# Attention steps of three score units on rotating pairs of PSUM banks, with a joined value phase for two query chunks, in a fused attention and gated-FFN kernel

## Chip, cores and metric

The kernel runs on one core of a Trainium2 chip. The metric is the time of one execution on the device in microseconds (us). "Before" is the kernel as it was and "after" the changed one. A comparison uses runs of both kernels on the same chip in the same rounds.

## The reference

Eight batches of causal attention (8 heads, 576 queries, 16 extra "beacon" keys that no mask covers, head size 64) are reshaped to 4608 tokens of 512 features and go through a gated feed-forward network (FFN) with 1536 hidden columns.

```python
B, H, S, Nb, D = (8, 8, 576, 16, 64)
scores = scale * np.matmul(q, k_all.transpose(0, 1, 3, 2))      # k_all: beacon keys, then keys
scores = np.where(causal, -1000000000.0, scores)
a = np.exp(scores - scores.max(-1, keepdims=True))
a /= a.sum(-1, keepdims=True) + 1e-09
x = np.matmul(a, v_all)        # then (B, H, S, D) -> (B*S, H*D)
gate = np.maximum(x @ w_gate, 0.0)
out = (gate * (x @ w_val)) @ w_out
```

## The kernel before

Attention of one batch and the FFN of earlier tokens run interleaved, so that TensorE always has matmuls while ScalarE (ACT) does exponentials and VectorE (DVE) multiplies and reciprocals. The work of a batch is cut into 14 score **units**: a tile of two PSUM banks, four to twenty matmuls, one exponential. A batch has seven **steps** of two units. When all units of a query chunk (of 240, 256 or 80 queries) are done, a **value phase** multiplies the exponentials by the values and sums them. Then a quota of FFN groups follows: "up" (four gate matmuls, Relu, four value matmuls, multiply) or "down" (twelve matmuls, copy out). What no batch is left to cover runs at the end as a **tail** of FFN alone, with 24 up groups.

PSUM, the memory that matmuls write to, has eight banks here, shared so: two score pairs (four banks), two banks for a value phase, two single banks for the FFN. The value matmuls of some up groups use the first bank of a score pair (`spare`).

```python
s_ps = main.enter_context(tc.tile_pool(name="s_ps", bufs=2, space=bass.MemoryType.PSUM))
o_ps = main.enter_context(tc.tile_pool(name="o_ps", bufs=1, space=bass.MemoryType.PSUM))
f_ps = main.enter_context(tc.tile_pool(name="f_ps", bufs=2, space=bass.MemoryType.PSUM))

class Unit:
    def qk(self):
        self.s = s_ps.tile([P, 2, 512], FP32, name="s")
        ...                                   # score matmuls into both banks
    def exp(self):
        e = psb.tile([P, 1024], BF16, name="e")
        nc.scalar.activation(e..., self.s..., AF.Exp, scale=scale)
        ...                                   # causal mask on GpSimd where needed

class Ffn:
    def up(self, nf, c0, c1, spare):
        g = f_ps.tile([P, M_TILE], FP32, name="f")
        for ki in range(KM):
            nc.tensor.matmul(g[:, :n], wg[:, ki, nf * P:(nf + 1) * P], x[:, ki], ...)
        gs = fsb.tile([P, M_TILE], FP32, name="g")
        nc.scalar.activation(gs[:, :n], g[:, :n], AF.Relu)
        if spare:
            u = s_ps.tile([P, 2, M_TILE], FP32, name="s")[:, 0]
        else:
            u = f_ps.tile([P, M_TILE], FP32, name="f")
        for ki in range(KM):
            nc.tensor.matmul(u[:, :n], wv[:, ki, nf * P:(nf + 1) * P], x[:, ki], ...)
        nc.vector.tensor_mul(self.h[:, nf, c0:c1], gs[:, :n], u[:, :n])

plan = (... + [(b, i, 2.6 if b == 2 else 4.4) for b in range(2, B) for i in range(7)]
        + [(None, 0, 4.5)])                   # batch, step, FFN quota

for s, (b, i, quota) in enumerate(plan):
    units = [Unit(batches[b], order[2 * i + x]) for x in range(2)]
    for j, u in enumerate(units):
        u.qk()
    units[0].exp()
    values()                                  # value phases that are due
    other = list(units[1:])
    for j, (kind, _, run) in enumerate(mine): # FFN groups within the quota
        run(spare)
        if other:
            other.pop().exp()                 # second exponential after the first group
```

The batches are counted from zero in the code: `b == 2` is the third batch.

Of the kernel before, what the change touches and what calls it, by code (L numbers as in the profile page):

```python
# [10 lines left out]
FP32 = mybir.dt.float32  # L11
# [5 lines left out]
def general_path(tc, q, k, v, beacon_k, beacon_v, out, ident, wg, wv, wo):  # L17
# [79 lines left out]
    with tc.tile_pool(name="gen_sb2", bufs=1) as sb, \  # L97
# [56 lines left out]
        ((g, 0, 0),), ((g, 0, 1), (g, 1, 3)), ((g, 1, 2),), ((g, 1, 1),), ((g, 1, 0),),  # L154
        ((g, 2, 4), (g, 2, 3), (g, 2, 2)), ((g, 2, 1), (g, 2, 0)))
)


@with_exitstack
def kernel(  # L160
# [12 lines left out]
    nc = tc.nc  # L173
# [27 lines left out]
    bounds = [const.tile([P, 256], FP32, name=n) for n in ("least", "most")]  # L201
# [10 lines left out]
    s_ps = main.enter_context(tc.tile_pool(name="s_ps", bufs=2, space=bass.MemoryType.PSUM))  # L212
    o_ps = main.enter_context(tc.tile_pool(name="o_ps", bufs=1, space=bass.MemoryType.PSUM))
    f_ps = main.enter_context(tc.tile_pool(name="f_ps", bufs=2, space=bass.MemoryType.PSUM))
# [111 lines left out]
    UNITS = [(x, t) for t in range(NKT) for x in "kqv"]  # L326
# [24 lines left out]
    class Unit:  # L351
# [9 lines left out]
        def qk(self):  # L361
            self.s = s_ps.tile([P, 2, 512], FP32, name="s")
            for g, _, (kt, q0, n, _, _), c in self.parts:
                (kT, k0), (qT, q0) = self.batch.keys(kt), self.batch.queries(q0)
                for j in range(2):
                    for a in range(2):
                        rows = slice(a * D, (a + 1) * D)
                        nc.tensor.matmul(  # L368
                            self.s[:, a, c + j * n:c + (j + 1) * n],
                            kT[rows, 2 * g + j, k0:k0 + P], qT[rows, 2 * g + j, q0:q0 + n],  # L370
                            start=True, stop=True)
# [17 lines left out]
    class Chunk:  # L389


        def __init__(self, batch, g, ci):
            self.batch, self.g, self.ci = batch, g, ci
            self.last = len(CHUNKS[ci][2]) - 1
            self.turned = batch.b == 0 and ci < 2

        def av(self):
            spare = self.batch.b == 0 and self.g == 1
            if spare and self.ci == 2:
                s = s_ps.tile([P, 2, 2, 256], FP32, name="s")  # L400
                self.ab, self.os = s[:, 0], s[:, 1, 0]
            else:
                self.ab = (f_ps if spare else o_ps).tile(
                    [P, 2, 256], FP32, name="f" if spare else "ab")
                self.os = (f_ps if spare else o_ps).tile(
                    [P, 256], FP32, name="f" if spare else "os")
            cq0, _, segs = CHUNKS[self.ci]
            order = sorted(segs, key=lambda x: x[0])
            for i, (kt, q0, n, _, _) in enumerate(order):
                e = self.batch.e.pop((self.g, self.ci, kt))  # L410
                kr = min(P, Stot - kt * P)
                for part in range(3):
                    for hh in range(4):
                        rows = slice(hh * C, (hh + 1) * C)
                        c0 = (4 * self.g + hh) * D + part * C
                        w = ones[:kr, :] if part == 2 else self.batch.v[:kr, kt, c0:c0 + C]
                        o = self.os[rows] if part == 2 else self.ab[rows, part]
                        nc.tensor.matmul(  # L418
                            o[:, q0 - cq0:q0 - cq0 + n], w, e[:kr, 2 * (hh % 2) + hh // 2],
                            start=(i == 0 and part != 1), stop=(i == self.last),  # L420
                            skip_group_check=True)
                        if self.turned and i == 0 and part == 2 and n < 256:
                            nc.tensor.matmul(o[:, n:], ones, ones[:, :256 - n],
                                             start=False, stop=True, skip_group_check=True)

        def invert(self):
            n = CHUNKS[self.ci][1]
            self.r = nrm.tile([P, 256], FP32, name="r")
            if not self.turned:
                nc.vector.reciprocal(self.r[:, :n], self.os[:, :n])  # L430
                return


            few = nrm.tile([P, 8], FP32, name="few", bufs=2)
            nc.vector.transpose(self.r, self.os)
            nc.vector.reciprocal(few, self.r[:, ::C])
            nc.vector.transpose(self.r.rearrange("p (b c) -> p b c", c=C),
                                few.unsqueeze(2).to_broadcast([P, 8, C]))

        def scale(self):  # L440
            cq0, n, _ = CHUNKS[self.ci]
            t0 = self.batch.b * S + cq0
            nc.vector.tensor_mul(xT[:, 2 * self.g:2 * self.g + 2, t0:t0 + n],  # L443
                                 self.ab[:, :, :n],
                                 self.r[:, :n].unsqueeze(1).to_broadcast([P, 2, n]))

        def note(self):
            n = CHUNKS[self.ci][1]
            for x, op in zip(bounds, (ALU.min, ALU.max)):
                nc.vector.tensor_tensor(out=x[:, :n], in0=x[:, :n], in1=self.r[:, :n], op=op)  # L450

    class Ffn:
# [4 lines left out]
        def up(self, nf, c0, c1, spare):  # L457
            n = c1 - c0
            if self.h is None:
                self.h = fsb.tile([P, NF, M_TILE], BF16, name="hT")  # L460
            x = xT[:, :, self.m0 + c0:self.m0 + c1]
            g = f_ps.tile([P, M_TILE], FP32, name="f")
            for ki in range(KM):
                nc.tensor.matmul(g[:, :n], wg[:, ki, nf * P:(nf + 1) * P], x[:, ki],  # L464
                                 start=(ki == 0), stop=(ki == KM - 1))
            gs = fsb.tile([P, M_TILE], FP32, name="g")
            nc.scalar.activation(gs[:, :n], g[:, :n], AF.Relu)  # L467
            if spare:
                u = s_ps.tile([P, 2, M_TILE], FP32, name="s")[:, 0]
            else:  # L470
                u = f_ps.tile([P, M_TILE], FP32, name="f")
            for ki in range(KM):
                nc.tensor.matmul(u[:, :n], wv[:, ki, nf * P:(nf + 1) * P], x[:, ki],  # L473
                                 start=(ki == 0), stop=(ki == KM - 1))
            nc.vector.tensor_mul(self.h[:, nf, c0:c1], gs[:, :n], u[:, :n])  # L475

        def down(self, ms):
            last = self.m0 + (ms + 1) * P == n_tokens
            for n0 in range(0, d_model, 256) if last else (0,):
                n = slice(n0, n0 + 256) if last else slice(0, d_model)  # L480
                o = f_ps.tile([P, d_model], FP32, name="f")
# [23 lines left out]
    def count_rows(ok):  # L505
        cnt_ps = o_ps.tile([1, 1], FP32, name="os")
        nc.tensor.matmul(cnt_ps, ok, ones[:, :1], start=True, stop=True)
        cnt = const.tile([1, 1], mybir.dt.int32, name="cnt")
        nc.vector.tensor_copy(cnt, cnt_ps)
        return cnt  # L510
# [3 lines left out]
    STEPS = 7  # L514
# [3 lines left out]
    BASE = [STEPS * b + sum(map(len, ALONE[:b])) for b in range(B)]  # L518

    plan = ([(0, i, 0) for i in range(STEPS)]  # L520
            + [(None, 0, n) for n in ALONE[0]]
            + [(1, i, 1) for i in range(STEPS)]
            + [(None, 0, n) for n in ALONE[1]]
            + [(b, i, 2.6 if b == 2 else 4.4) for b in range(2, B) for i in range(STEPS)]
            + [(None, 0, 4.5)])

    with tc.manual_schedule():
# [14 lines left out]
        idle_ps = o_ps.tile([P, M_TILE], FP32, name="os")  # L542
# [123 lines left out]
        after(s2 - 2, lambda: load_w(wg, moe_w_gate, 1152, 1536))  # L666
        after(s2 - 2, lambda: load_w(wv, moe_w_val, 1152, 1536))
        after(s2 - 1, lambda: load_wo(0, 6))
# [17 lines left out]
        def close_wide():  # L686
            wide_ctx.close()
            pools["osb"] = main.enter_context(tc.tile_pool(name="osb", bufs=6))

        after(s2 + 1, close_wide)  # L690

        def fetch(b, s0, late=1):
            at(s0, lambda: batches.update({b: Batch(b)}))
            for j, u in enumerate(UNITS):
# [5 lines left out]

        fetch(2, s2, 3)
        fetch(3, BASE[3] - STEPS - 2, 2)
        for b in range(4, B):
            fetch(b, BASE[b] - STEPS)

# [11 lines left out]
        for s, (b, i, quota) in enumerate(plan):  # L717
# [9 lines left out]
            if b is not None:  # L727
                if i == 0:
                    batches[b].e = {}
                order = (UNITS_FIRST, UNITS_BY_CHUNK)[b] if b < 2 else UNITS_BY_GROUP  # L730
                units = [Unit(batches[b], order[2 * i + x]) for x in range(2)]
# [11 lines left out]
            for j, u in enumerate(units):  # L743
                u.qk()
# [15 lines left out]
            if s == STEPS:  # L760
# [13 lines left out]
            other = list(units[1:])  # L774
# [27 lines left out]
            while len(notes) > (6 if s < s2 else 2):  # L802
                notes.pop(0)()
            for u in units:
                for g, ci, _, _ in u.parts:
                    left = [x for un in (order[2 * i + 2:]) for x in un if x[:2] == (g, ci)]
                    if not left and not any(c.g == g and c.ci == ci for c in due):
                        due.append(Chunk(batches[b], g, ci))
                        done = [x for un in order[2 * i + 2:] for x in un if x[1] == ci]
                        if not done:  # L810
                            ready[s + 2] = b * S + CHUNKS[ci][0] + CHUNKS[ci][1]
        run_sp()
# [46 lines left out]
```

## Time and profile before

| | before |
|---|---|
| time, median of 3 runs | 391.26 us (389.34 to 391.3) |
| profiled span, mean granted clock | 389.1 us, 0.995 |
| TensorE busy | 374.1 us, 96% |
| one later batch (160.16 to 200.71 us) | 40.55 us |
| tail (321.84 to the end) | 67.3 us, 24 up groups |

The prediction below shows the busy shares, the chain and a step. Three more lines of the page matter. The first is the clock granted to TensorE in 40 slices, in tenths; the others are groups of instructions: line, engine, operation, result and inputs, count, then busy us, mean ns of one, and the idle time ahead of them with what ended it.

```profile
PEclk9999989999999999999999999999999999999999
...
L464 PE MATMUL f<-xT,wg 128*128 128x512 bf16 x432 | 112.2, 382 | 0.3 <-DMA hwide<-in_k_dram 0.3
...
L473 PE MATMUL s<-xT,wv 128*128 128x512 bf16 x240 | 61.6, 379 | 0.0
```

In front of gate matmuls (L464) TensorE idled 0.3 us in the whole run, in front of the value matmuls that land in a score pair 0.0.

### The profile page before, as it was taken

The numbers are of one execution on the slowest core, as the hardware profiler recorded it, in microseconds if no ns is written. First come the engines' busy times: TensorE is split into PE (matmuls) and PEld (weight loads), VectorE is DVE, ScalarE is ACT, GpSimd is POOL, SyncE is SP. The second block draws the span as 40 slices with busy tenths as digits, with TensorE's granted clock in tenths as the row PEclk, the third lists the DMA queues.
The fourth block names the chain that finished last, engine by engine and source line by source line (L and its number), as shares of the span: only waits on it lengthen the run. The fifth ranks groups of instructions, "written<-read, shape, count | busy, mean of one in ns | idle before, by whom it ended". The sixth has DMA issues, their size and how long they took to land.

```text
span 389.1 us, 10272 instructions
## 1 busy us (share of the span) xinstructions
PE 374.1 (96%) x4297; PEld 187.4 (48%) x4297; DVE 204.3 (53%) x342; ACT 192.9 (50%) x270; POOL 127.8 (33%) x220
## 2 busy tenths in 40 slices
PE   7889889998999999999999999999999999999995
PEld 3554435543554545545544545445545454444443
DVE  4767456543566566465547653757266635512420
ACT  4763556336555554565546554655466533323321
POOL 1597284334462462253414351435021100000000
PEclk9999989999999999999999999999999999999999
DMA  8999999979996996499449933993300020011002
GB/s 215 215 186 178 200 199 210 166 174 174 215 161 164 188 183 125 115 203 172 101 128 193 182 86 106 197 203 77 98 29 2 2 83 29 0 52 59 0 29 87
DMA packets 148132, 50.44 MB, mean 130 GB/s; under 512 B 133616, under 2 KB 143600, under 8 KB 148080
## 3 DMA queue, kind: packets, MB, share of 16 engines
q1 hardware_dynamic: 139024, 44.48, 57.2%
q0 software_dynamic: 9056, 5.24, 9.8%
q8 instruction: 35, 0.57, 0.7%
q14 instruction: 17, 0.14, 0.1%
HBM read 38.34 MB, written 9.44 MB: 123 GB/s over the span
## 4 chain that ended last, share of the span: by engine, by line
PE 75%; DMA 12%; SPq 6%; POOL 4%; issue 1%; DVE 1%; ACT 0%; POOLq 0%; DVEq 0%
PE f L483 22%; PE f L464 21%; PE s L473 11%; PE f L473 9%; PE ab L418 6%; PE s L368 5%; DMA raw<-in_v_dram 5%; DMA raw<-in_k_dram 2%; PE os L418 2%; SPq L244 2%; DMA wv<-in_moe_w_val_dram 2%; SPq L268 2%; SPq L281 1%; DMA qT<-half 1%; POOL e L384 1%
## 5 line engine op out<-in xcount | busy, mean ns | idle before, releaser
L376 ACT ACTIVATE e<-s 128x1024 bf16<-128x1024 f32 (+2 forms) x112 | 104.9, 963 | 25.3 <-PE s L368 25.3
L464 PE MATMUL f<-xT,wg 128*128 128x512 bf16 x432 | 112.2, 382 | 0.3 <-DMA hwide<-in_k_dram 0.3
L467 ACT ACTIVATE g<-f 128x512 f32<-128x512 f32 x108 | 64.5, 597 | 84.6 <-PE f L464 82.6
L483 PE MATMUL f<-wo,hT 128*128 128x512 bf16 (+1 forms) x444 | 96.7, 374 | 0.0
L384 POOL TENSOR_SCALAR_AFFINE_SELECT e<-e 128x512 bf16<-128x512 bf16 (+2 forms) x80 | 46.8, 597 | 135.6 <-ACT e L376 127.6
L430 DVE RECIPROCAL r<-os 128x80 f32<-128x80 f32 (+2 forms) x43 | 57.6, 1339 | 57.0 <-PE os L418 57.0
L475 DVE TENSOR_TENSOR hT<-g,s 128x512 bf16<-128x512 f32 x60 | 41.2, 687 | 66.4 <-PE s L473 65.3
L473 PEld LDWEIGHTS <-wv 128*128 128x128 bf16 x432 | 42.3, 98 | 53.3 <-issue 3.0
L483 PEld LDWEIGHTS <-hT 128*128 128x128 bf16 x444 | 41.9, 98 | 47.3
L464 PEld LDWEIGHTS <-wg 128*128 128x128 bf16 x432 | 39.6, 98 | 46.8 <-issue 1.7
L473 PE MATMUL s<-xT,wv 128*128 128x512 bf16 x240 | 61.6, 379 | 0.0
L486 ACT COPY ob<-f 128x512 f32<-128x512 f32 (+1 forms) x37 | 21.3, 575 | 73.9 <-PE f L483 71.9
L475 DVE TENSOR_TENSOR hT<-g,f 128x512 bf16<-128x512 f32 x48 | 33.0, 688 | 36.6 <-PE f L473 32.0
L473 PE MATMUL f<-xT,wv 128*128 128x512 bf16 x192 | 49.8, 381 | 0.6 <-DMA wv<-in_moe_w_val_dram 0.4
L263 POOL CAST half<-raw 128x512 bf16<-128x512 f32 (+2 forms) x60 | 37.4, 634 | 31.0 <-DMA raw<-in_k_dram 11.3
L418 PE MATMUL ab<-e,v 128*32 128x80 bf16 (+4 forms) x1320 | 39.3, 233 | 3.8 <-POOL e L384 3.8
L368 PE MATMUL s<-qT,kT 64*128 64x80 bf16 (+3 forms) x704 | 35.8, 235 | 1.8 <-ACT e L376 1.0
L418 PEld LDWEIGHTS <-v 128*32 128x32 bf16 (+1 forms) x1408 | 26.5, 97 | 13.6 <-issue 9.0
L259 POOL CAST v<-raw 128x512 bf16<-128x512 f32 (+1 forms) x40 | 26.5, 664 | 19.3 <-DMA raw<-in_v_dram 19.3
L368 PEld LDWEIGHTS <-kT 64*128 64x128 bf16 x704 | 20.3, 96 | 25.8 <-issue 23.7
L418 PE MATMUL os<-e,ones 128*32 128x240 bf16 (+4 forms) x660 | 32.2, 232 | 0.0
L443 DVE TENSOR_TENSOR xT<-ab,r 128x480 bf16<-128x480 f32 (+2 forms) x45 | 24.9, 554 | 0.8
(66 smaller groups left out, 134.7 us busy)
## 6 DMA issues: line engine op xcount, KB each, us to landing
out_dram<-ob SPq DMA_DIRECT2D x35, 256.0 KB, 2.1
raw<-in_q_dram SPq DMA_DIRECT2D x25, 256.0 KB, 4.8
raw<-in_v_dram SPq DMA_DIRECT2D x24, 256.0 KB, 5.0
raw<-in_k_dram SPq DMA_DIRECT2D x19, 256.0 KB, 4.3
raw<-in_v_dram SPq DMA_DIRECT2D x8, 224.0 KB, 4.2
wo<-in_moe_w_out_dram POOLq DMA_DIRECT2D x2, 768.0 KB, 9.9
raw<-in_k_dram SPq DMA_DIRECT2D x6, 224.0 KB, 4.5
raw<-in_v_dram SPq DMA_DIRECT2D x8, 160.0 KB, 4.3
```

Of the source, the lines that this page charges most:

```text
L259: copy(self.v[:n, t].rearrange("p (h a d) -> p h a d", a=2, d=C), raw[:n].rearrange("p (h d a) -> p h a d", a=2, d=C))
L263: copy(h[:n], raw[:n])
L368: nc.tensor.matmul(self.s[:, a, c + j * n:c + (j + 1) * n], kT[rows, 2 * g + j, k0:k0 + P], qT[rows, 2 * g + j, q0:q0 + n], start=True, st ...
L376: nc.scalar.activation(e[:, :k * 4 * n].rearrange("p (k a x) -> p a k x", k=k, a=2), self.s[:, :, :k * 2 * n].rearrange("p a (k x) -> p a ...
L384: nc.gpsimd.affine_select(out=cols[:, :, :m], in_=cols[:, :, :m], pattern=[[0, 4], [1, m]], compare_op=ALU.is_ge, fill=0.0, base=base, cha ...
L418: nc.tensor.matmul(o[:, q0 - cq0:q0 - cq0 + n], w, e[:kr, 2 * (hh % 2) + hh // 2], start=(i == 0 and part != 1), stop=(i == self.last), sk ...
L430: nc.vector.reciprocal(self.r[:, :n], self.os[:, :n])
L464: nc.tensor.matmul(g[:, :n], wg[:, ki, nf * P:(nf + 1) * P], x[:, ki], start=(ki == 0), stop=(ki == KM - 1))
L467: nc.scalar.activation(gs[:, :n], g[:, :n], AF.Relu)
L473: nc.tensor.matmul(u[:, :n], wv[:, ki, nf * P:(nf + 1) * P], x[:, ki], start=(ki == 0), stop=(ki == KM - 1))
L475: nc.vector.tensor_mul(self.h[:, nf, c0:c1], gs[:, :n], u[:, :n])
L483: nc.tensor.matmul(o[:, n], self.h[:, nf, ms * P:(ms + 1) * P], wo[:, nf, n], start=(nf == 0), stop=(nf == NF - 1))
```

## The change

From the third batch on, 14 units go in steps of 3, 3, 3, 3 and 2, so that kinds of matmul alternate less often. The score pairs and the FFN banks are merged into three rotating pairs: each unit, up group and down group takes the next pair (but the first unit of a step without a value phase takes the two value banks), and an up group has gate and value in the two banks of one. The first and last query chunk share one value phase with one reciprocal of 320 columns. The order of the units in a batch changes with it. Keys and queries are fetched before values, and some weight loads move one step later.

```diff
-    s_ps = main.enter_context(tc.tile_pool(name="s_ps", bufs=2, space=bass.MemoryType.PSUM))
     o_ps = main.enter_context(tc.tile_pool(name="o_ps", bufs=1, space=bass.MemoryType.PSUM))
-    f_ps = main.enter_context(tc.tile_pool(name="f_ps", bufs=2, space=bass.MemoryType.PSUM))
+    ps_ctx = ExitStack()
+    s_ps = ps_ctx.enter_context(tc.tile_pool(name="s_ps", bufs=2, ...))
+    f_ps = ps_ctx.enter_context(tc.tile_pool(name="f_ps", bufs=2, ...))
...
+        def join_banks():                       # called at the first step of the third batch
+            ps_ctx.close()
+            pools["p"] = main.enter_context(tc.tile_pool(name="p_ps", bufs=3, ...))
+    def pair():
+        return pools["p"].tile([P, 2, 512], FP32, name="p")
...
-            g = f_ps.tile([P, M_TILE], FP32, name="f")
+            if "p" in pools:
+                both = pair()
+                g, u = both[:, 0], both[:, 1]
+            else:
+                g, u = f_ps.tile([P, M_TILE], FP32, name="f"), None
             ...                                 # gate matmuls
             nc.scalar.activation(gs[:, :n], g[:, :n], AF.Relu)
-            if spare:
+            if u is not None:
+                pass
+            elif spare:
...
-            + [(b, i, 2.6 if b == 2 else 4.4) for b in range(2, B) for i in range(STEPS)]
+            + [(2, i, n) for i, n in enumerate((2, 2, 1, 1, 1))]
+            + [(b, i, 6.2) for b in range(3, B) for i in range(5)]
...
-        fetch(2, s2, 3)
-        fetch(3, BASE[3] - STEPS - 2, 2)
-        for b in range(4, B):
-            fetch(b, BASE[b] - STEPS)
+        fetch(2, s2 + 1, 2)
+        for b in range(3, B):
+            fetch(b, BASE[b] - 5)
...
             for j, u in enumerate(units):
-                u.qk()
+                if len(units) > 2 and not chunks and j == 0:
+                    u.qk(o_ps.tile([P, 2, 512], FP32, name="o"))
+                else:
+                    u.qk()
...
+            if len(units) > 2:
+                for u in units[1:]:
+                    u.exp()                     # all three ahead of the FFN
...
-                        due.append(Chunk(batches[b], g, ci))
+                    cis = (ci,) if b < 2 or ci == 1 else (0, 2)
+                        due.append(Chunk(batches[b], g, cis))
```

## The prediction

> **What bounds the kernel now.** I read the page from the top: busy shares first, then the chain that ended last, then the waits of the TensorE matmul row.
>
> ```profile
> PE 374.1 (96%) x4297; PEld 187.4 (48%) x4297; DVE 204.3 (53%) x342; ACT 192.9 (50%) x270; POOL 127.8 (33%) x220
> ...
> PE 75%; DMA 12%; SPq 6%; POOL 4%; issue 1%; DVE 1%; ACT 0%; POOLq 0%; DVEq 0%
> ```
>
> TensorE is the bound: 96% busy, 75% of the chain. The DMA, queue and Pool parts of the chain all lie before 119 us (the chain in order of time); after that it is matmuls alone. In the list of who waited for whom, the only TensorE wait above 1.5 us is for masks on GpSimd (3.8 us in 3 waits, all before 96 us). One step of the fifth batch shows how tight the rest is:
>
> ```profile
> 160.16 1.04 PE L464 MATMUL f<-xT,wg 128*128 128x512 bf16 x4
> 161.03 1.03 PE L473 MATMUL s<-xT,wv 128*128 128x512 bf16 x4
> 161.23 0.60 ACT L467 ACTIVATE g<-f 128x512 f32<-128x512 f32 x1 [0.70 <-PE f L464]
> 161.90 1.03 PE L464 MATMUL f<-xT,wg 128*128 128x512 bf16 x4
> 162.17 0.69 DVE L475 TENSOR_TENSOR hT<-g,s 128x512 bf16<-128x512 f32 x1 [1.21 <-PE s L473]
> 162.76 1.03 PE L473 MATMUL f<-xT,wv 128*128 128x512 bf16 x4
> 163.72 0.61 PE L368 MATMUL s<-qT,kT 64*128 64x256 bf16 x8
> 163.90 0.69 DVE L475 TENSOR_TENSOR hT<-g,f 128x512 bf16<-128x512 f32 x1 [0.81 <-PE f L473]
> 164.26 0.39 PE L418 MATMUL ab<-e,v 128*32 128x240 bf16 x8
> 164.85 1.04 PE L464 MATMUL f<-xT,wg 128*128 128x512 bf16 x4
> ```
>
> Columns are start, time, engine, line, operation. Two things matter. (1) An FFN "up" group is four gate matmuls and four value matmuls; the value ones start 0.86 us after the gate ones (161.03, then 161.90, then 162.76), with no gap, although ACT's Relu of the gate bank runs from 161.23 to 161.83. They can, since gate and value are separate PSUM tiles. (2) A change between scores, values and FFN costs little: eight score matmuls of 256 columns, two at a time, stream for 8 x 256 / 2 / 2.4 GHz = 0.43 us and took 0.54 (163.72 to 164.26), so about 0.11 us a change.
>
> **What the Trainium skill says.** (a) "PSUM — Partial Sum Buffer", section "PSUM bank collisions raise a hardware error": guard PSUM by bank and quadrant; engines on different banks run cleanly. So no hazard asks a value matmul to wait for a Relu on the other bank. The trace agrees: 161.03 against 161.23 above. (b) "Perfetto Trace Analysis", section "Optimizing Tensor Performance", Matmuls: independent groups should rotate through PSUM banks so that one's evacuation overlaps the next one's matmuls. The trace shows that overlap. (c) "TensorE: Matmul & The Clock Gate", Part 3: matmuls start and end in program order, so nothing fills the engine behind a held matmul. In the trace the matmuls of the next line never pass a held one. (d) The same page, Part 1: the clock halves after an idle window of about 3.4 us. The trace agrees, by stretches of 2 us (columns: length, then busy us of PE, PEld, DVE, ACT, POOL, then the granted clock, DMA, GB/s):
>
> ```profile
> 20.00:22.00 2.00, 1.14 (x40) 0.87 (x36) 1.75 (x4) 1.77 (x3) 1.99 (x4) 1.00 0.90 245
> 48.00:50.00 2.00, 0.06 (x3) 0.09 (x1) 1.17 (x2) 1.90 (x3) 1.85 (x3) 1.00 0.96 220
> 52.00:54.00 2.00, 2.00 (x7) 0.71 (x6) 1.88 (x2) 1.11 (x2) 1.99 (x4) 0.50 1.16 173
> ```
>
> 57% busy kept full clock; a nearly empty stretch led to half clock for some 3.5 us.
>
> **The change part by part.** I compared the two compiled instruction orders and traced every semaphore wait back to the instruction that reaches its count. Matmul numbers are equal.
>
> *Fewer changes between kinds of work.* Batches three to eight go from seven steps to five, and value phases from six to four per batch. In the compiled order the kernel's own part has 33 fewer runs of one kind: 33 x 0.11 = **3.6 us saved**.
>
> *Feeding batch three and four.* Keys and queries are fetched first, values last; the weight loads come later. The old wait for masks near 93 us and for a transposed query at 118 us (about 2.5 us together) should go, since fewer loads are needed by each step and TensorE will be slower: **2.5 us saved**. Elsewhere before 70 us I assume no net change, plus or minus 2.
>
> *The pair as one tile.* This decides it. An up group now takes one tile of two banks, gate in bank 0, value in bank 1. Dependencies are kept per tile: in the compiled order the first value matmul of a group waits for an ACT count, and that count is the Relu **of the same group**. I counted 89 such waits among the 108 up groups, every one from the third batch on, tail included. In the kernel before, value matmuls that wait for a Relu wait only for an older one that is long done.
> Cost of one: gate start to Relu start 1.07 us (160.16 to 161.23), Relu 0.60, release to matmul 0.06 (an exponential that ends near 21.48 lets the scores start at 21.54). So the value matmuls start 1.73 us after the gate ones, not 0.86: 0.87 us held, in which TensorE has nothing else. 89 x 0.87 = **77.4 us added**. None of it hides: TensorE is the bound, and the next gate matmuls stand behind in order.
>
> *Exponentials ahead of the first Relu.* The steps of three units put all three exponentials (1.02 us of 128x1024, 0.97 of 128x960) on ACT before the first Relu. In a step with a value phase TensorE is away long enough. In the second step of each batch there is none: after two down groups, ACT copies for 0.6 us, then runs three exponentials until about 3.76 us after the step began; Relu and release make 4.42, while the gate matmuls ended at 1.70: 2.7 us held, 1.83 more than counted. Five batches: 9.2 us. The first two steps of batch three: about 3 us.
>
> *The third score unit.* With three pairs in rotation it takes the pair of the last FFN group of the step before. After an up group, multiply start to release is 0.28 + 0.69 + 0.06 = 1.03 us after the last matmul (162.76 + 0.86 = 163.62, then 163.90); the unit is due at 0.46 to 0.54. About 0.5 us held in two steps a batch and 0.3 after a down group in a third: 1.36 x 5 = 6.8 us, and 1.3 in batch three.
>
> *Joined first and last chunk.* One reciprocal of 320 columns in place of 240 and 80 (1650 and 657 ns; about 2.2 us by their slope): off the path on a DVE 53% busy.
>
> **Sum:** 391.3 - 3.6 - 2.5 + 77.4 + 12.2 + 8.1 = 482.9; with a little for clock loss, **484 us**, 24% slower.
>
> **Rivals.** *The intended gain.* If the value matmuls didn't wait, the result would be 391.3 - 6 + some 20 of pair and ACT waits, less what hides: 385 to 405 us. For it: banks differ, so the chip needs no wait, and it is what the author intends. Against: the wait stands in the compiled stream, and the count it names is the Relu's. I leave 4% for having misread it.
> *The clock drops.* The second steps hold TensorE 2.7 us at a stretch, and every up group runs 1.73 busy in 2.6 us. For: the half clock after 48 us. Against: 57% busy kept full clock, and 2.7 is shorter than 3.4. If the long holds did it, 5 to 7 times 1.5 us, towards 495; if the 66% duty did, far beyond 550.
> *DMA becomes the bound.* Batch three now has 7 FFN groups in place of 9 while the next batch is fetched. Against: every batch takes about 13 us longer, so transfers only gain slack. Nothing.
> *ACT becomes the bound.* It was 50% busy; its work does not grow. It is no throughput bound, though its latency now lies on the path in every up group.
>
> **Range and chances.** 89 waits with 0.03 us of doubt each give 3 us; the step-start terms perhaps 8; the clock 0 to 12. Range 472 to 500. Faster 2%, within 2% of before 2%, slower 96%.
>
> **What would show each step.** Right: PE's busy share falls to about 77 to 80%, and a new wait of value matmuls for the Relu tops TensorE's list, near 89 times, some 85 us in total, most singly 0.87 and a few 2 to 3 us; scores waiting for DVE's multiply 10 to 15 times of about 0.5; in the tail, gate to gate 2.6 us in place of 1.73; ACT's Relu enters the chain. ACT's and DVE's busy us stay within 2%. Wrong: no such wait and 1.73 us per up group in the tail; or PEclk tenths below 9 after 120 us, which would mean that the clock is the larger cost; or DMA shares at 1.0 after 120 us.

## The result and the profile after

After took **484.06 us** (median of four runs, 483.55 to 484.77) against 390.67 us before (four runs, 389.34 to 391.3). The ratio is 1.2397, 95% interval 1.2357 to 1.2438. Ratios here are the mean time of one kernel's runs over that of the other's of the same rounds, so not quite the ratio of the medians quoted.

The page of after: busy shares, granted clock, shares of the chain, and the costliest group.

```profile
PE 391.1 (81%) x4297; PEld 189.7 (39%) x4297; DVE 199.7 (41%) x306; ACT 191.1 (40%) x270; POOL 124.2 (26%) x220
...
PEclk8799899999999998999999998999999999999999
...
PE 67%; ACT 16%; DMA 6%; POOL 3%; issue 3%; SPq 2%; DVE 2%; DVEq 0%; POOLq 0%; ACTq 0%
...
L504 PE MATMUL p<-xT,wv 128*128 128x512 bf16 x356 | 92.8, 383 | 69.0 <-ACT g L496 69.0
```

TensorE's share falls from 96 to 81%, ACT enters the chain with 16%, and the zero in front of the value matmuls has become 69.0 us. No engine has more work: TensorE has the same 4297 matmuls, and ACT's busy time is 191.1 us against 192.9. (Most of the 17.0 us that TensorE's busy time grew by is how the profile counts a matmul's end, see below: an estimated 89 x 0.17 = 15 us.) Two slices past 100 us show a clock of 8 tenths.

Who waited for whom on TensorE, with total us, times, and the longest:

```profile
PE p L504 <- ACT g L496: 69.0, 89, 2.1
PE p L381 <- DVE hT L506: 4.6, 13, 0.5
PE f L504 <- DMA wv<-in_moe_w_val_dram: 2.3, 2, 1.7
```

Value matmuls (L504) wait for a Relu (L496) 89 times. Two groups of the tail, in time order (start, us, engine, line, operation, idle before), show which Relu:

```profile
422.22 0.60 ACT L496 ACTIVATE g<-p 128x512 f32<-128x512 f32 x1 [2.17 <-PE p L493]
...
422.87 1.02 PE L504 MATMUL p<-xT,wv 128*128 128x512 bf16 x4 [0.68 <-ACT g L496]
...
423.73 1.03 PE L493 MATMUL p<-xT,wg 128*128 128x512 bf16 x4
...
424.79 0.60 ACT L496 ACTIVATE g<-p 128x512 f32<-128x512 f32 x1 [1.97 <-PE p L493]
425.44 1.02 PE L504 MATMUL p<-xT,wv 128*128 128x512 bf16 x4 [0.68 <-ACT g L496]
```

The gate matmuls start at 423.73, their Relu runs from 424.79 to 425.39, and only then, at 425.44, do the value matmuls of the same group start: 1.71 us after the gate ones, where the kernel before took 0.86. The profile names 0.68 us of idle time, not 0.85, because it models the end of a matmul row some 0.17 us after its last column has streamed (1.03 us for a row whose successor starts after 0.86). So the 89 waits for the own Relu cost an estimated 89 x 0.85 = 75.7 us. The 69.0 us of the list is less, although it also holds the longer waits of the second steps, told next.

The second step of a batch is different. These are ACT and TensorE rows of one, and two stretches of 2 us (length, busy us of PE, PEld, DVE, ACT and POOL, granted clock, DMA share, GB/s):

```profile
181.95 1.03 ACT L389 ACTIVATE e<-o 128x1024 bf16<-128x1024 f32 x1
182.11 1.04 PE L493 MATMUL p<-xT,wg 128*128 128x512 bf16 x4
182.86 1.84 ACT L389 ACTIVATE e<-p 128x960 bf16<-128x960 f32 x2
184.56 0.63 ACT L496 ACTIVATE g<-p 128x512 f32<-128x512 f32 x1
185.25 1.75 PE L504 MATMUL p<-xT,wv 128*128 128x512 bf16 x4 [2.10 <-ACT g L496]
186.78 1.91 PE L493 MATMUL p<-xT,wg 128*128 128x512 bf16 x4
```

```profile
184.00:186.00 2.00, 0.76 (x3) 0.32 (x3) 0.00 (x0) 1.19 (x2) 2.00 (x5) 0.85 0.97 227
186.00:188.00 2.00, 2.00 (x6) 0.69 (x5) 0.69 (x1) 0.00 (x0) 0.92 (x2) 0.50 1.33 228
```

Three exponentials stand on ACT ahead of the Relu, so the value matmuls start 3.14 us after the gate ones (185.25 - 182.11). After that hold TensorE got half its clock: the next two rows of four matmuls take 1.75 and 1.91 us in place of 1.03.

Last, the third score unit waits for the pair that an up group before it still holds through DVE's multiply:

```profile
208.38 0.61 PE L381 MATMUL p<-qT,kT 64*128 64x256 bf16 x12
208.56 0.69 DVE L506 TENSOR_TENSOR hT<-g,p 128x512 bf16<-128x512 f32 x1 [1.88 <-PE p L504]
...
209.30 0.38 PE L381 MATMUL p<-qT,kT 64*128 64x240 bf16 x4 [0.30 <-DVE hT L506]
```

One steady batch adds these up. The stretches run from the score matmuls of one step to those of the same step a batch later; with the view held to the Relu line the columns are length, ACT's busy us in it (count), clock, DMA share, GB/s. First before, then after:

```profile
160.16:200.71 40.55, 7.17 (x12) 1.00 0.78 147
```

```profile
195.48:249.49 54.01, 7.20 (x12) 0.97 0.50 110
```

A batch has 12 up groups and takes 13.46 us more. The parts: 12 x 0.85 = 10.2 own-Relu holds; 1.41 more in the second step (3.13 from gate to value less the 1.72 of a first group in other steps); 1.28 for half clock there (that step's four up groups took 13.08 us against 10.39 in other steps, so 2.69 in all, less 1.41); 1.34 for the third unit (worked out in experiment 6); less an estimated 33 / 5 x 0.11 = 0.73 for fewer changes of kind. Sum 13.5.

### The profile page after: what moved, and what is told of

Its sections match the earlier page's. It is cut to its first block, busy times and chain, and to the rows that moved or that the text cites. A ratio compares the mean times of both kernels' runs of the same rounds, so it can differ in the third digit from the quotient of the medians.

```text
span 482.2 us, 10234 instructions
## 1 busy us (share of the span) xinstructions
PE 391.1 (81%) x4297; PEld 189.7 (39%) x4297; DVE 199.7 (41%) x306; ACT 191.1 (40%) x270; POOL 124.2 (26%) x220
## 4 chain that ended last, share of the span: by engine, by line
PE 67%; ACT 16%; DMA 6%; POOL 3%; issue 3%; SPq 2%; DVE 2%; DVEq 0%; POOLq 0%; ACTq 0%
PE p L504 19%; PE p L514 17%; PE p L493 15%; ACT g L496 11%; PE o L438 6%; ACT e L389 4%; DMA wo<-in_moe_w_out_dram 3%; DMA raw<-in_v_dram 3%; PE f L514 2%; PE p L381 2%; DVE hT L506 2%; PE f L493 2%; PE s L504 1%; ACT ob L517 1%; POOL e L397 1%
## 5 line engine op out<-in xcount | busy, mean ns | idle before, releaser
L504 PE MATMUL p<-xT,wv 128*128 128x512 bf16 x356 | 92.8, 383 | 69.0 <-ACT g L496 69.0
L506 DVE TENSOR_TENSOR hT<-g,p 128x512 bf16<-128x512 f32 x89 | 61.2, 688 | 188.1 <-PE p L504 186.2
L496 ACT ACTIVATE g<-p 128x512 f32<-128x512 f32 x89 | 53.4, 600 | 144.8 <-PE p L493 144.3
L504 PEld LDWEIGHTS <-wv 128*128 128x128 bf16 x432 | 42.0, 98 | 139.7 <-issue 97.2
L493 PE MATMUL p<-xT,wg 128*128 128x512 bf16 x356 | 94.0, 387 | 0.1
L514 PE MATMUL p<-wo,hT 128*128 128x512 bf16 (+1 forms) x396 | 85.5, 373 | 0.0
L389 ACT ACTIVATE e<-p 128x1024 bf16<-128x1024 f32 (+2 forms) x77 | 68.8, 962 | 25.3 <-PE p L381 25.3
L451 DVE RECIPROCAL r<-o 128x256 f32<-128x256 f32 (+3 forms) x31 | 55.8, 1799 | 49.0 <-PE o L438 49.0
L438 PE MATMUL o<-e,v 128*32 128x80 bf16 (+4 forms) x1320 | 38.2, 233 | 1.9 <-POOL e L397 1.4
L438 PEld LDWEIGHTS <-v 128*32 128x32 bf16 (+1 forms) x1408 | 27.4, 98 | 10.2 <-issue 7.3
L389 ACT ACTIVATE e<-s 128x1024 bf16<-128x1024 f32 (+2 forms) x28 | 25.6, 963 | 9.2 <-PE s L381 9.2
L493 PE MATMUL f<-xT,wg 128*128 128x512 bf16 x76 | 20.5, 390 | 0.9 <-DMA wg<-in_moe_w_gate_dram 0.6
## 6 DMA issues: line engine op xcount, KB each, us to landing
wo<-in_moe_w_out_dram POOLq DMA_DIRECT2D x2, 768.0 KB, 11.8
```

The source lines that it names most:

```text
L389: nc.scalar.activation(e[:, :k * 4 * n].rearrange("p (k a x) -> p a k x", k=k, a=2), self.s[:, :, :k * 2 * n].rearrange("p a (k x) -> p a ...
L438: nc.tensor.matmul(o[:, q0 - cq0:q0 - cq0 + n], w, e[:kr, 2 * (hh % 2) + hh // 2], start=(x == 0 and i == 0 and part != 1), stop=stop, ski ...
L451: nc.vector.reciprocal(self.r[:, :self.n], self.os[:, :self.n])
L514: nc.tensor.matmul(o[:, n], self.h[:, nf, ms * P:(ms + 1) * P], wo[:, nf, n], start=(nf == 0), stop=(nf == NF - 1))
```

## The experiments

Twelve kernels ran. All outputs are right. The theory: the cost is the pair taken as one tile, which makes value matmuls wait for their own group's Relu, plus ACT's order and the pair's late release. The rivals: a loss of clock from the thinner duty, and the rearranged fetches.

### 1. The Relu behind the value matmuls

```diff
-            nc.scalar.activation(gs[:, :n], g[:, :n], AF.Relu)
+            if u is None:
+                nc.scalar.activation(gs[:, :n], g[:, :n], AF.Relu)
             ...                                      # value matmuls
+            if "p" in pools:
+                nc.scalar.activation(gs[:, :n], g[:, :n], AF.Relu)
             nc.vector.tensor_mul(self.h[:, nf, c0:c1], gs[:, :n], u[:, :n])
```

> The changed kernel with one move: the Relu of an up group is issued after the value matmuls of the group in place of before them, so that the value matmuls of the shared pair no longer wait for it. Theory (the wait for the own Relu, 89 times 0.865 us, plus the slow first Relu and half clock in the second steps): no such wait left in the trace, and the time falls by 77 us for the waits and some 10 to 13 us for the second steps, to 392 to 399 us. What stays above 391 would be the third score unit's waits (about 7 to 9 us) and the later weight loads (2 to 3 us) less 3.6 us for fewer changes of work. Rival (the five steps, the three pairs or the fetches cost most of it): it stays above 430 us.

Measured: **406.41 us** (404.83 to 407.47) against 391.98 before, ratio 1.0368 (1.0342 to 1.0394). The edit moves one ACT instruction per group in the issue order, adds nothing, and takes away 77.6 of the 93 us. That settles the main cause. The 77.6 is a net figure: it also holds the second steps' share, less a new loss. So the expectation of 392 to 399 was missed by 7. In the waits of TensorE in this run:

```profile
PE p L381 <- DVE hT L509: 5.7, 7, 0.9
PE p L381 <- ACT e L389: 4.9, 6, 0.8
```

Relu and multiply now both run after the value matmuls, so a pair comes free later, and the third unit waits longer for it: about 2.3 us a batch by its phases in the timeline, where after has 1.34. Part of the saving came back there.

### 2. The same in the tail alone

The edit is that of experiment 1, done only for the last queue of groups.

> The same move only in the last stretch, after attention, where 24 up groups run with no exponentials and no score units about: a dose. Theory: 24 times 0.865 us = 20.8 us less than the changed kernel, 463.3 us, gate to gate 1.73 us there and 2.57 us in the attention steps as before. Rival (the wait is hidden or something else sets the pace of up groups): less than 10 us gained.

Measured: **464.75 us** (463.96 to 465.6), ratio 1.1839 (1.1812 to 1.1867). The 24 tail groups are worth 484.06 - 464.75 = 19.3 us, or 0.80 each; 463.3 was expected. The tail has no attention and no exponentials, and little DMA, so the other parts of the change have nothing to act on there. (From 321.84 us to the end before and from 395.24 after, the tail grew from 67.3 to 87.0 us; in the trace of this run it takes 66.7.) The wait is down to the groups outside the tail:

```profile
PE p L505 <- ACT g L497: 53.6, 65, 2.3
```

### 3. The kernel before with one pair per tail group

```diff
+            if pools.get("tail"):
+                both = s_ps.tile([P, 2, M_TILE], FP32, name="s")
+                g, u = both[:, 0], both[:, 1]
```

> The kernel before with nothing of the change but this: in the last stretch the gate and value halves of an up group lie in one tile of two banks, the score pair that is free by then. Theory: the false wait alone costs 24 times 0.865 us, 390.7 + 20.8 = 411.5 us (22 of the 24 name their own Relu in the compiled order; with 22 it is 409.7). Rival (it takes the rest of the change to make the wait bite): under 395 us.

Measured: **410.76 us** (408.25 to 411.2) against 391.98, ratio 1.0452 (1.041 to 1.0494): 18.8 us more. Its wait list and two rows of its tail:

```profile
PE s L476 <- ACT g L468: 15.3, 22, 0.9
```

```profile
351.40 0.60 ACT L468 ACTIVATE g<-s 128x512 f32<-128x512 f32 x1 [1.98 <-PE s L465]
352.05 1.02 PE L476 MATMUL s<-xT,wv 128*128 128x512 bf16 x4 [0.69 <-ACT g L468]
```

22 waits, 18.8 / 22 = 0.85 us each. Put into the old kernel alone, the shared tile makes the same wait (0.69 us as the profile counts it). The matmuls, the Relu and the number of banks per group are those of the kernel before; only the tile that they are declared in is wider.

### 4. The exponentials spread over the FFN groups

```diff
-            if len(units) > 2:
-                for u in units[1:]:
-                    u.exp()
-            other = units[1:] if len(units) == 2 else []
+            other = units[1:]              # one popped (in order) after each FFN group
```

> The changed kernel with the exponentials of the second and third score unit issued after the first and second FFN group in place of before the first. The waits for the own Relu stay. Theory: the holds of 2.3 us at the first up group of the second steps shrink to about 0.9, and the stretches of half clock after them go, 2.7 us a batch in four or five batches and less in two: 10 to 14 us less than the changed kernel, 470 to 474 us. Rival (half clock comes from the 66 per cent duty of up groups, not from the long hold): the half clock stays, and less than 6 us are gained.

Measured: **472.3 us** (470.92 to 473.48), ratio 1.2035 (1.1996 to 1.2074): 11.8 us less than after by the medians, 14 by the ratios ((1.2397 - 1.2035) x 391.5). The wait for the Relu keeps its count but no longer has long members:

```profile
PE p L504 <- ACT g L496: 62.2, 89, 0.9
```

The mean clock rose from 0.975 to 0.992, and after 61 us the trace shows no half clock at all, where after has three stretches of 3.41 us. The up groups still run at two thirds duty, so half clock followed the long hold, not the duty.

### 5. The third unit behind the value phase

This is experiment 1, and the third unit's score matmuls go after the value phase where there is one (`if j == 2 and chunks: values()` ahead of `u.qk()`).

> Relu after the value matmuls (as in the first experiment, 406.4 us), and in steps of three score units with a value phase the third unit is issued after the value phase. Theory: what held that kernel 14 us above the kernel before is above all the third score unit, which takes the pair of the last FFN group and waits until its Relu and multiply are done: the trace shows the score phases of those steps at 1.67 and 1.79 us for 0.56 and 0.64 us of streaming, about 2.4 us a batch. A value phase of 1.1 us in between covers it: 12 us less in holds, 1.8 us more for 16 further changes of work, 395 to 397 us. Rival (the pair rotation holds the next FFN group in place of the score unit, so the hold only moves): over 402 us.

Measured: **396.57 us** (394.46 to 397.93) against 391.93, ratio 1.0099 (1.0064 to 1.0133). So 10 of the 14 us by which experiment 1 stayed above before were the third unit's. What stays shows in the waits: 3.8 us once for a transposed query, 3.1 for the value weights in two waits.

### 6. The third unit late, alone

Only the edit of experiment 5, on after, with the Relu where after has it.

> The changed kernel with only the third score unit moved behind the value phase; Relu stays ahead of the value matmuls. It prices the third term of the prediction by itself. Prediction's term: 8.1 us of holds there, less 1.8 us for 16 further changes of work: 6.3 us less, 477.8 us. The trace of the changed kernel names 4.6 us of such waits: with that, 2.8 us less, about 481.3 us. If under 1 us is gained the term was an error.

Measured: **476.07 us** (475.94 to 476.87), ratio 1.214 (1.2111 to 1.2168): 8.0 us less than after, more than either expectation. Of the 13 waits of scores for DVE's multiply one is left, of 0.5 us. The timeline gives 1.01 us a batch as the net saving: the score rows of the three steps concerned take 1.24, 1.23 and 1.06 us in after, and 0.80, 0.86 and 0.86 here with the extra change of kind (0.11 each, hence 1.01 + 0.33 = 1.34 of waiting in after). That is 5 us in all. In the profiled runs the rest is mostly clock: here only one of the second steps took 13.08 us and the others 11.80. But three further runs of this kernel had a mean clock of 0.976 to 0.977, like after, and took the same 475.94 to 476.87 us, so the split between hold and clock is not shown for them. The hold itself was as long:

```profile
PE p L504 <- ACT g L496: 71.7, 89, 2.3
```

Why fewer of them lost the clock can be read from the traces. In each of the 14 traces the stretches of half clock start on a grid of 3.413 us (each trace has its own offset) and, between 20 us and the end of the kernel, last one or two of its periods: in after they start at 55.69, 185.40, 240.01 and 294.63 us, 38, 16 and 16 periods apart. What separates the periods that are followed by half clock is how long TensorE idles within one. Three periods of this run (length, TensorE's busy us, granted clock, DMA share, GB/s):

```profile
181.29:184.70 3.41, 1.34 (x7) 1.00 1.03 255
184.70:188.11 3.41, 2.73 (x8) 0.50 0.73 138
...
232.49:235.90 3.41, 1.64 (x28) 1.00 0.85 227
```

The hold from 181.05 to 183.36 us fell almost whole into the first period, and the next got half the clock. The hold from 234.13 to 236.44 was as long, but a new period began at 235.90, and the clock stayed at 1.00. Counted over the 14 traces from 20 us to some 8 us before the end, by the profile's idle times: after each of the 24 periods that idled 2.07 us or more at full clock the next ran at half, after none of the 1555 that idled 1.82 or less; of the four between, two were followed by half clock. So it is partly luck whether a given hold costs clock.

### 7 and 8. Loads and fetches

First the weight loads back where before has them, on top of experiment 5:

> The same, with the last third of the two FFN weights and the output weights loaded where the kernel before loads them. Theory: in the changed kernel TensorE waits for those weights between 50 and 56 us, 2.3 us of it by name and the rest at half clock, of which the kernel before loses about half: 1 to 2.5 us less than the previous run, some 394 us. Rival (the values of the second batch are then late in their place and hold TensorE just as long): within 0.7 us of it.

Measured: **395.1 us** (392.6 to 396.77), ratio 1.0069 (1.0031 to 1.0108): 1.5 us less, but the intervals of the two runs overlap. Then in addition the fourth batch fetched two steps earlier, its casts one step later after the load (`BASE[b] - (7 if b == 3 else 5), 2 if b == 3 else 1`):

> The same again, with the fetch of the fourth batch begun two steps earlier, as in the kernel before. Theory: with Relu no longer in the way the fourth batch reaches its second step before its queries are turned (2.6 us wait for a transposed query at 122 us in the first experiment's trace): that wait goes, 2 to 3 us less, about 391 to 392 us, level with the kernel before. Rival (the earlier fetch delays the third batch's own data): no gain.

Measured: **392.56 us** (390.64 to 395.42) against 391.93, ratio 1.0008 (0.9965 to 1.0052), the same as before. Three later batches with 12 up groups each take 40.17 us in its trace against 40.55: 16 fewer changes of kind over five batches predict 16 x 0.11 / 5 = 0.35. The intended gain is real and is 0.4 us a batch. About as much is lost earlier, in waits such as 5.5 us for masks in this profile against 3.8 before; that part differs from run to run, and its cause isn't settled by these two runs.

### 9. The bank plan of before with steps of three

Experiment 8 without the merged pairs: two score pairs and two single FFN banks throughout, and so the Relu ahead of the value matmuls again, as in before.

> Five score steps of three units and the joined value phase of first and last chunk, but on the bank plan of the kernel before: two score pairs and two single FFN banks, no Relu or FFN tile in a pair that a later FFN tile waits for. The third unit is issued after the value phase, as in the run where that alone was joined with the late Relu. If the cost was the sharing of pairs alone, all holds go and only 16 fewer changes of matmul kind remain (157 phases against 173): 16 x 0.11 = 1.8 us less than the kernel before, some 390 us (388.5 to 391.5). Rival: three units on two pairs bring a new wait, the third unit behind the first unit's exponential of the same step, or the early part loses some us as in the other runs with the same fetches: 392 to 396 us.

Measured: **400.86 us** (400.2 to 403.58) against 392.2, ratio 1.023 (1.0198 to 1.0261). A miss, and one for both parts of the expectation. A batch takes 42.07 us (158.15 to 200.22). The second step shows where:

```profile
166.93 1.84 ACT L389 ACTIVATE e<-s 128x960 bf16<-128x960 f32 x2
167.05 1.03 PE L505 MATMUL f<-xT,wv 128*128 128x512 bf16 x4
168.63 0.63 ACT L497 ACTIVATE g<-f 128x512 f32<-128x512 f32 x1
169.31 1.02 PE L493 MATMUL f<-xT,wg 128*128 128x512 bf16 x4 [1.24 <-ACT g L497]
```

The value matmuls (167.05) no longer wait. But with two FFN banks the *next* gate matmuls need the bank that the Relu reads, and that Relu still stands behind three exponentials. So the issue order on ACT costs time on either bank plan; with pairs it comes on top of the own-Relu wait.

### 10 and 11. The joined value phase alone

The kernel before with its seven steps and banks, and only first and last chunk joined (with the unit order, the order of loads and the fetch of the third batch as in after):

> The kernel before with its seven steps of two score units and its bank plan, and of the change only the joined value phase of first and last query chunk: 165 phases against 173, 8 fewer x 0.11 = 0.9 us less than before, some 390.5 us. If the early part's losses come from the order of loads and fetches and not from the joined phase, the same as before within 0.5%; if the joined phase itself waits for something (its longer run of value matmuls holds the wide value bank), 392 us or more.

Measured: **399.66 us** (399.04 to 400.41), ratio 1.0185 (1.0161 to 1.0209), a miss. One later batch took 40.34 us, 0.21 less than before, as expected; but another of equal work took 40.58 (199.53 to 240.10 us), so that gain is not shown. The loss is in the third batch, where the new unit order puts a masked unit right ahead of the value phase that needs it:

```profile
PE o L438 <- POOL e L397: 8.2, 4, 3.4
```

Two of these waits, 2.4 us at 101.0 and 3.45 at 120.7 us, were not there before, and half clock followed the second. So the third batch was given back the order, chunks and fetches of before, and all later batches the old order of loads (`LOADS_BEFORE`, `OLD = 9`):

> The run with seven steps and the joined chunk alone (399.66 us) lost its time in the third batch: its value phases waited 2.4 and 3.45 us for masks, with half clock after the second, while from one later batch to the next it was 0.2 us shorter than before (40.34 against 40.55). Here the third batch keeps the unit order, chunks and fetches of the kernel before, and the joined chunk starts with the fourth. If the order in the third batch caused the loss, it goes whole: 390 to 391.5 us, 0.5 to 1 below before. If the loss comes from the merged wide value tile, which both have, it stays near 399.

Measured: **394.17 us** (391.72 to 395.71) against 392.53, ratio 1.0024 (0.9977 to 1.0072): most of the loss is gone, and the wide value tile, which both runs have, did not cause it. Which of the things given back did is not shown; the masks of the third batch are what the wait list names. The expected 390 to 391.5 was not reached. The runs at 391.7 to 391.8 us had a clock of 0.991 and 0.994, that at 395.7 had 0.978; a gain of 1 us is smaller than this scatter.

### 12. Steps of three, old banks, spread exponentials

> Third batch as in the kernel before; from the fourth on five steps of three units on the bank plan of before, and the exponentials of second and third unit issued behind the first and second FFN group. The run with the old banks took 42.07 us a batch against 40.17 with pairs and late Relu; if its extra 1.9 us are gate matmuls of the second group held by a Relu behind three exponentials (1.24 us named by the profile in each batch), spreading them brings the batch to 40.1 to 40.3 us and the whole to 389 to 391.5 us. If two score pairs are too few for three units whatever the order, the batch stays at 41 to 42 us and the whole at 393 to 398.

Measured: **398.39 us** (397.51 to 398.7), ratio 1.0142 (1.0101 to 1.0183). A batch is 40.49 us (244.06 to 284.55) in place of 42.07, so the wait of experiment 9 was ACT's order and not the number of pairs; it lies between the two expectations, 0.2 us above what was hoped. The whole missed for a new reason in the fourth batch:

```profile
PE o L389 <- DVE xT L475: 3.0, 1, 3.0
```

In a step without a value phase the first unit takes the value tile (`o`), and there it waited 3.0 us for DVE to finish the reciprocal and scaling of the phase before; half clock followed (TensorE's next row of four took 1.91 us). No version of the twelve beats the kernel before; experiments 8 and 11 equal it within the scatter.

## Why the prediction was right, point by point

- **The total.** The mechanism was right. That 484 us and 484.06 agree to 0.1 is luck: the own-Relu waits were 1.7 us below the forecast, and the gain of 2.5 us from feeding did not show.
- **The pair as one tile, +77.4.** Right. The wait has 89 members as counted, and gate to value takes 1.71 us where 1.73 was forecast: 75.7 us. Experiment 1 moves the Relu alone and the time falls by a net 77.6 us, experiment 2 shows 0.80 per group in the tail, and experiment 3 produces it in the old kernel at 0.85. The forecast of "some 85 us" in the wait list was too high, since the list showed 69.0: the profile counts idle time from the modelled end of a matmul.
- **Exponentials ahead of the first Relu, +12.2.** The mechanism is right, its division was not. The extra hold was 1.41 us in four of the five batches and 0.54 in the other, not 1.83: ACT's first exponential began 0.59 us after the step where 0.8 follows from the prediction's numbers, and consecutive operations of ACT overlap by about 0.1 us in the trace (182.86 against an end at 182.98). Half clock after it, which the prediction kept as a rival of "0 to 12", added 1.3 to 1.6 us in three of these steps. With the third batch it is about 12 us; experiment 4 takes away 12 to 14.
- **The third score unit, +8.1.** Right in the main: 1.34 us a batch by the timeline (1.36 predicted), 13 waits of at most 0.5 us. Experiment 6 takes away 8.0 us, more than the 6.3 that follow, with some clock in it.
- **Fewer changes of kind, -3.6.** Right in its unit, 0.11 us, as far as experiment 8 shows: its later batches are 0.38 us shorter where 0.35 follow from it. Experiment 10 leaves it open (0.21 us shorter in one batch, none in the next, where 0.18 follow). The 2.4 GHz in its working is what the trace shows: 2048 columns of a row of four in 0.86 us.
- **Feeding batch three and four, -2.5, and no net change before 70 us.** Not shown. The start of the FFN-alone stretch came 2.8 us later (79.15 against 76.36), a little outside the 2 allowed; 0.5 of it was there at 46.5 us, and the rest came later, where after waits for weights (2.3 us above) and before for masks (2.2). The stretch from there to the tail grew by 70.6 us, while 65 x 0.85 + 12 + 6.8 - 3.6 = 70.5 is the sum without this term, so nothing of it shows.
- **The rivals.** The intended gain didn't happen. Duty alone did not lower the clock: in the tail, 396 to 404 us had 5.93 us busy and clock 1.00. The long holds did, in three of the five second steps. The prediction set this aside because "2.7 is shorter than 3.4", and there it misread its own trace, which it says agrees with an idle window of 3.4 us: TensorE's idle time ahead of the half clock at 51.03 us was one wait of 2.15 us (48.06 to 50.22). DMA did not become the bound (its share fell from 0.78 to 0.50 in a later batch). ACT is no throughput bound at 40%, yet it holds 16% of the chain.
- **The signs.** One sign of being wrong came: PEclk tenths of 8 after 120 us, in two slices. The clock was still not the larger cost, some 4 of 93 us. TensorE's share came out at 81%, just above the "77 to 80" named, gate to gate in the tail at 2.57 us (2.6 named). DVE's busy time fell by 2.3%, a little more than the 2% named. The joined reciprocals gave 1.8 us of that (57.6 to 55.8; 2.16 us for 320 columns where 240 and 80 took 1.65 and 0.66), and the updates of the smallest and largest reciprocal are joined too (72 instructions in place of 96).

## What to carry to other kernels

Before two banks go into one tile, ask which engine reads the first while another writes the second: dependencies go by the tile, and a read of one half can order a write of the other, group after group. Where a shared tile is wanted, issue all writes before the first read, but then ask who takes the buffer next and when it comes free. (Not run: the rotating pair declared as two tiles of one bank each, with the Relu left where it was.) On an in-order engine off the critical path the order of issue decides as much as the load: put the small operation that a bound engine waits for ahead of large ones that nobody needs yet.

## What the Trainium skill lacked or had wrong

- "TensorE: Matmul & The Clock Gate", Part 1, "What's actually happening" and "A second HAM failure mode: psum-queue depth-cycling": half clock is tied to an idle window of about 3.4 us, or to frequent short idles between groups of 512-column matmuls. Here periods of 3.41 us do show, but one need not be idle throughout: 2.10 us of idle time in one was enough (181.99 to 185.40 us in after: 1.31 us busy, then clock 0.50), so a hold of 2.1 us is not safe as a reader would take it to be. The short idles did nothing: with 0.68 us ahead of each row of value matmuls in the tail the clock was 1.00, and after the 1.24 us of experiment 9 too.
- The same page, "Back-to-back issue gap", gives about 131 ns per matmul of 512 columns in a stream. Here four take 0.86 us in every dense stretch, 216 ns each, which is the figure that this section calls the isolated gap and that the page's Part 1 measures for back-to-back matmuls.
- No page says that a tile of two banks can couple them, although the banks themselves are free: 89 waits, an estimated 76 us here.
- "Perfetto Trace Analysis" says that the end of a matmul is estimated by the profiler, but no page says how far that shortens the idle time shown: 0.69 us was named where 0.85 was lost.
